# Q, K and V of three chunks as 64-row matmul pairs inside the gate-up stages of a fused adaLN, local-attention and GLU block

## Chip, cores and metric

The kernel runs on one core of one Trainium2 chip. The metric is the device time of one execution in microseconds (us). Three runs of the kernel before took 559.21, 559.87 and 560.19 us; the median is 559.87.

## What is computed

```python
x = A_x                                          # 1 x 2048 x 576, bfloat16
mod = (silu(c) @ w_mod).reshape(1, 6, 1, 576)
sa, ca, ga, sb, cb, gb = mod[:, 0], ..., mod[:, 5]
h = layernorm(x) * (1 + ca) + sa
q, k, v = h @ wqkv                               # 32 heads of 18
# each position attends to 8 positions: itself and those 2, 4, ... 14 before it
attn = softmax(mask(q . k[pos - 2*w] * 18**-0.5))
x = x + ga * ((attn . v[pos - 2*w]) @ wo)
h = layernorm(x) * (1 + cb) + sb
x = x + gb * (((h @ w_gate) * (h @ w_up)) @ w_down)   # 576 -> 4608 -> 576
```

## The kernel before

The 2048 rows are 8 chunks of 256 (`CH`), or 16 tiles of 128. The attention half works by chunks; the feed-forward half works by five groups of tiles, `GROUPS = [(0, 2), (2, 6), (6, 10), (10, 13), (13, 16)]` (L42). The width 576 is held as four blocks of 128 rows and one of 64 (`KF`, index 4).

**The stages.** After a prologue (chunk 0, and Q, K, V of chunks 1 and 2) the loop at L1066 runs, for each group `gi`, `gate_up(gi)` (L651) and then `down(gi)` (L713). In the texts, "gate-up 1" is the gate-up stage of group 1, the second one. PE carries the stage's own matmuls; the attention of later chunks is woven in as *pieces*, small functions that issue some instructions. Each engine runs its instructions in the order in which the code issues them: the schedule is written by hand. `spread` (L641) places the pieces over the loop by their weights: a piece goes to the loop count `f` in which the middle of its weight falls.

**Gate-up** (L651 to L700) loops over 36 blocks `f` of 128 of the 4608 columns. For each it forms a gate tile `pg` and an up tile `pu`, each in a PSUM bank of its own. It uses matmuls with 64 rows of contraction: one on the array's lower 64 rows and one on its upper 64 rows run at the same time. 576 rows are nine halves of 64, so each tile takes nine 64-row matmuls. `first_part(f)` issues five pairs: lower rows write `pg`, upper rows `pu`; the odd half comes from `wgr`, which holds the last 64 weight rows of gate in its lower and those of up in its upper half. `second_part(f)` issues the other four pairs with the banks swapped. Before it a wait makes sure that the last matmul of the first part has landed, as the two halves must not write one bank together (L676). The order is `first_part(f)`, `second_part(f - 1)`, the pieces of `f`, `product(f - 1)`, so that a first part lies between the two parts of one `f`. ACT copies `pu` and `pg` to `u_sb` and `g_sb` (L683, L684, three buffers each); DVE multiplies them into `hh` (L688). `ahead` (L702) asks for the weight block two blocks on, on SP's queue.

**Down** (L713 to L779) loops over the same 36 blocks and accumulates, for each tile `j` of the group, a 512-wide matmul into `acc` (L726) and a 64-wide one into `accr` (L730). The first 32 loops carry pieces, all of weight 1. The `wd` blocks come by POOL's queue, three buffers. The outputs are scaled, added and stored at the end.

**A chunk's attention, in pieces.**
- `a_ln`, `a_norm` (L337, L342): statistics on DVE, `rsq` on ACT (Ln, Exp), the norm on DVE into `ln_xn`. The norm also writes the last 64 columns a second time, beside the first copy.
- `a_t` (L357), called T: ten PE transposes into two banks, then scale and shift on DVE and ACT into `hT`.
- `a_q` (L386): Q and K as nine tiles of 128 columns, five full-array matmuls of 256 columns each (L376); ACT copies them to `qT` and `kT`, of which there are two sets, and copies 16 halo columns of the chunk before (`a_halo`). The fifth block of Q and of K share one tile, with weights `wq4`.
- `a_v` (L394): V for each of two tiles, five matmuls 504 wide and five 72 wide; ACT copies them with the order of head and element exchanged (`v_sb`), and POOL's queue writes them to DRAM (`vd`). In the fifth block of rows the upper 64 weight rows are zero.
- `b_ld` (L412): POOL's queue reads eight shifted copies of V back from DRAM.
- `b_p`, `b_lq`, `b_lt`, `b_sm0`, `b_sm1`: products of Q and shifted K on DVE, sums over a head on PE, transposes, softmax. `b_mul`, `b_add`: weighted sum of V on DVE.
- `b_o`, `b_w`, `b_ln`, `b_norm`, `b_t`: transposes, `wo`, residual, second norm, transposes into `h2T`, which the next gate-up reads.

**Where they stand.** Gate-up 1, 2 and 3 carry the middle of the attention of chunks 3 and 4, 5 and 6, and 7 (`gbg`, L1041). A down stage carries, from `out_qkv(i, n)` (L630), the end of chunk `i` mixed with the norm, T, Q, K and V of chunk `n`. Down 0 does so for n = 3 and 4, down 1 for n = 5 and 6, down 2 for n = 7 (`dbg`, L1062). `load_x(n + 2)` on SP's queue stands behind `a_norm(n)`.

**PSUM.** All tiles share one pool of eight banks; a tile waits until its bank's former tile has been read.

Of the kernel before, what the change touches and what calls it, by code (L numbers as in the profile page):

```python
# [7 lines left out]
BF = mybir.dt.bfloat16  # L8
# [30 lines left out]

MODK = (0, 4, 1, 2, 3)  # L40
QKK = (0, 1, 4, 2, 3)
GROUPS = [(0, 2), (2, 6), (6, 10), (10, 13), (13, 16)]  # L42


@with_exitstack
def kernel(
# [47 lines left out]
    def js(j):  # L94
        return slice(j * P, (j + 1) * P)
# [193 lines left out]
    def transposed(src, dst, cols, vi, between=None):  # L289
        n = P * len(cols)  # L290
        pA = ps([P, 3, n], BF, "tr_pA")
        pB = ps([P, 2, n], BF, "tr_pB")
        for c, j in enumerate(cols):
            if c and between:
                between()
            for m in range(KT):
                d = pA[:, m, :] if m < 3 else pB[:, m - 3, :]
                nc.tensor.transpose(d[:, js(c)], src[:, j, m * P:(m + 1) * P], ident[:])  # L298

        def evict(on_dve=(0, 1, 2)):  # L300
            for m in range(KT):
# [55 lines left out]
    def a_t(i, on_dve=(0, 1, 2), between=None):  # L357
        a_tiles(i)
        hT = aa[i]["hT"]
        transposed(aa[i]["xn"], lambda m: hT[:, m, :], (0, 1), 0, between)(on_dve)  # L360

    def qk_w(kt, m):
        if m == KF:
# [80 lines left out]
    def b_lt(i):  # L444
        b = bb[i]
        lgs = b.pop("lgs")
        pt = ps([P, 2, ST, P], BF, "lt")
        for a in range(2):
            for j in range(ST):
                nc.tensor.transpose(pt[:, a, j, :], lgs[:, a, js(j)], ident[:])  # L450
        nc.scalar.copy(b["lgt"][:].rearrange("p a j w h -> p (a j w h)"), pt[:].rearrange("p a j n -> p (a j n)"))

    def b_sm0(i):
        b = bb[i]
        lg = b.pop("lgt")
        mx = smp.tile([P, ST, 4, H], BF, name="mx", tag="tree")
        dd = smp.tile([P, 2, ST, 4, H], F32, name="dd")
        nc.vector.tensor_tensor(mx[:], lg[:, 0], lg[:, 1], ALU.max)
        nc.vector.tensor_tensor(mx[:, :, 0:2], mx[:, :, 0:2], mx[:, :, 2:4], ALU.max)
        nc.vector.tensor_tensor(mx[:, :, 0], mx[:, :, 0], mx[:, :, 1], ALU.max)  # L460
        for wq in range(2):
            nc.vector.tensor_tensor(dd[:, wq], lg[:, wq], mx[:, :, 0:1].to_broadcast([P, ST, 4, H]), ALU.subtract)
        nc.scalar.activation(dd[:], dd[:], ACTF.Exp, scale=scale)
        b["dd"] = dd
# [32 lines left out]
    def b_o(i):  # L497
# [8 lines left out]
            nc.scalar.copy(oT[:, m:m + 2, :], pA[:, m:m + 2, :])  # L506
        nc.scalar.copy(oT[:, 4, :], pB[:, 0, :])

    keyed = []

    def to_keys(j):
# [102 lines left out]
    def B_two(a, b, av_a, av_b):  # L614
        return (B_pr(a, 0, 6) + B_lq(a, 0) + B_pr(a, 6, 8) + B_pr(b, 0, 2) + B_lq(a, 1) + B_pr(b, 2, 6) + B_lq(b, 0) + B_sm(a)
                + B_pr(b, 6, 8) + av_a[:4] + B_lq(b, 1) + av_a[4:] + B_sm(b) + av_b)

    def B_one(a, av_a):
        return B_pr(a, 0, 6) + B_lq(a, 0) + B_pr(a, 6, 8) + B_wait(1.5) + B_lq(a, 1) + B_wait(4.0) + B_sm(a) + av_a

    def B_av(i):
        r = []
# [6 lines left out]

    def out_qkv(i, n):  # L630
        o = [lambda: b_o(i), lambda: b_w(i, 0), lambda: b_w(i, 1), lambda: b_ln(i), lambda: b_norm(i), lambda: b_t(i, (0,) if i == 6 else (0, 1))]
        if n >= NCH:
# [15 lines left out]
        return at  # L648


    def gate_up(gi, hh, bg):  # L651
        N = P * (GROUPS[gi][1] - GROUPS[gi][0])
        ht = h2T[gi]
        at = spread(bg, FT)
        lo, hi = slice(0, 64), slice(64, P)
        pgu = {}

        def half(bank, lhs, rhs, first, last):
            return nc.tensor.matmul(bank[:, 0:N], lhsT=lhs, rhs=rhs, start=first, stop=last, skip_group_check=True)  # L659

        def first_part(f):
            wb = wgu_blk[gi * NBLK + f // FB]
            cs = slice((f % FB) * P, (f % FB + 1) * P)
            pg, pu = ps([P, 2 * CH], F32, "pg"), ps([P, 2 * CH], F32, "pu")
            half(pg, wgr[lo, js(f)], ht[lo, KF, 0:N], True, False)
            half(pu, wgr[hi, js(f)], ht[hi, KF, 0:N], True, False)
            for k in range(KF):
                half(pg, wb[lo, k, 0, cs], ht[lo, k, 0:N], False, False)
                m = half(pu, wb[hi, k, 1, cs], ht[hi, k, 0:N], False, False)
            pgu[f] = (pg, pu, m)  # L670

        def second_part(f):
            wb = wgu_blk[gi * NBLK + f // FB]
            cs = slice((f % FB) * P, (f % FB + 1) * P)
            pg, pu, m = pgu.pop(f)
            swap = nc.tensor.nop()  # L676
            tc.add_manual_dep(swap.ins, m.ins.name, SYNC, reason="row tiles swap banks")
            for k in range(KF):
                half(pu, wb[lo, k, 1, cs], ht[lo, k, 0:N], False, k == KF - 1)
                half(pg, wb[hi, k, 0, cs], ht[hi, k, 0:N], False, k == KF - 1)  # L680
            g = gup.tile([P, 2 * CH], BF, name="g_sb")
            u = gup.tile([P, 2 * CH], BF, name="u_sb")
            nc.scalar.copy(u[:, 0:N], pu[:, 0:N])  # L683
            nc.scalar.copy(g[:, 0:N], pg[:, 0:N])  # L684
            return g, u

        def product(f, gu):
            nc.vector.tensor_tensor(hh[:, f, 0:N], gu[0][:, 0:N], gu[1][:, 0:N], ALU.mult)  # L688

        for f in range(FT):  # L690
            first_part(f)
            gu = second_part(f - 1) if f > 0 else None
            if f > 0 and f % FB == 0:
                ahead(gi, f // FB)
            for piece in at[f]:
                piece()
            if gu:
                product(f - 1, gu)
        product(FT - 1, second_part(FT - 1))
        ahead(gi, NBLK)  # L700

    def ahead(gi, n):  # L702
# [352 lines left out]
    def gb_row():  # L1055
# [3 lines left out]
        b_ld(2, 1)  # L1059
        load_wd(2)  # L1060

    dbg = {0: [gb_row] + first + out_qkv(2, 4),  # L1062
           1: out_qkv(3, 5) + out_qkv(4, 6),
           2: out_qkv(5, 7) + out_qkv(6, 8),
           3: [nop, lambda: b_t(6, (1,))] + out_qkv(7, 8)}
    for gi in range(NG):  # L1066
        if gi == 1:
            hh0_guard.__exit__(None, None, None)
            wgx_guard.__exit__(None, None, None)
            hhp = pool("hhp", 1)  # L1070
        hh = hhp.tile([P, FT, 2 * CH], BF, name="hh") if gi else hh0
        gate_up(gi, hh, gbg.get(gi, []))
        down(gi, hh, dbg.get(gi, []))


# [28 lines left out]
```

## Time and profile before

| | |
|---|---|
| median of three runs | 559.87 us |
| profiled execution | 560.52 us |
| its span, first to last instruction | 558.7 us |
| granted PE clock | 1.00 |
| gate-up 0, down 0 | 49.7 to 92.0, 92.0 to 133.5 us |
| gate-up 1, down 1 | 133.5 to 207.4, 207.4 to 266.05 us |
| gate-up 2, down 2 | 266.05 to 339.9, 339.9 to 390.2 us |
| gate-up 3, down 3 | 390.2 to 445.0, 445.0 to 475.4 us |
| gate-up 4, down 4 | 475.4 to 528.15, 528.15 to 558.7 us |

All times within the trace are in us from the start of the span. The engines are PE (matmuls; PEld is its weight loads), DVE, ACT, POOL and SP. In the rows by instruction the first number is the start, the second the duration. A matmul's duration runs until its results have landed, so durations of matmuls in a row overlap: the time that one takes from PE's stream is the distance from its start to the next start. `64*128 64x512` means 64 contraction rows, 128 columns of weights, and 512 columns streamed.

### The profile page before, as it was taken

How to read it: one execution, taken by the hardware profiler on the slowest of the kernel's cores; microseconds unless marked ns; L12 is line 12 of the kernel's file. 1: busy time of each engine (PE TensorE's matmuls, PEld its weight loads, DVE VectorE, ACT ScalarE, POOL GpSimd, SP SyncE). 2: the span in 40 equal slices, each digit the busy share in tenths (PEclk: the TensorE clock that was granted, in tenths of full speed). 3: DMA queues.
4: the chain of work that ended last, by engine and by line, in shares of the span. 5: the costliest groups of instructions: out<-in, count | busy, mean ns of one | idle time of the engine just before them, and what ended most of it. 6: DMA issues, size and time to landing. Idle time of an engine off the chain costs nothing.

```text
span 558.7 us, 14224 instructions
## 1 busy us (share of the span) xinstructions
PE 547.8 (98%) x5972; PEld 325.0 (58%) x6012; DVE 331.2 (59%) x796; ACT 250.6 (45%) x584; POOL 63.4 (11%) x97
## 2 busy tenths in 40 slices
PE   7999999999999999999999999999999999999997
PEld 4887796665444446656444445655565555555564
DVE  7888798984777776252858686406736614322202
ACT  2746666354465652323355654230466511456500
POOL 3103101123000001111100000111100022000020
PEclk9999999999999999999999999999999999999999
DMA  8999999645646745233834855234965565565053
GB/s 271 282 292 309 340 306 352 193 147 177 230 143 218 247 141 166 92 101 106 288 119 152 276 174 182 86 106 128 324 195 192 185 194 177 182 193 187 1 170 117
DMA packets 69994, 108.14 MB, mean 194 GB/s; under 512 B 3658, under 2 KB 57754, under 8 KB 69930
## 3 DMA queue, kind: packets, MB, share of 16 engines
q1 hardware_dynamic: 58672, 61.28, 35.2%
q0 software_dynamic: 11168, 45.81, 25.4%
q8 instruction: 47, 0.77, 0.6%
q14 instruction: 17, 0.14, 0.1%
q10 hardware_dynamic: 90, 0.15, 0.1%
HBM read 102.78 MB, written 4.44 MB: 192 GB/s over the span
## 4 chain that ended last, share of the span: by engine, by line
PE 84%; DMA 10%; issue 3%; SPq 1%; DVE 1%; POOL 0%; POOLq 0%
PE pg L659 26%; PE pu L659 21%; PE acc L726 20%; PE pq L376 4%; PE accr L730 4%; DMA wgr<-in_B_w_gate_dram 3%; PE pw L577 2%; PE pv L399 2%; DMA wo<-in_A_wo_dram 2%; DMA wgu<-in_B_w_up_dram 2%; DMA x_t<-in_A_x_dram 2%; PE lg L434 2%; DMA wd<-in_B_w_down_dram 1%; SPq L150 1%; DMA wmA<-in_w_mod_dram 1%
## 5 line engine op out<-in xcount | busy, mean ns | idle before, releaser
L659 PE MATMUL pg<-h2T,wgu 64*128 64x512 bf16 (+2 forms) x1440 | 277.3, 333 | 0.0
L659 PE MATMUL pu<-h2T,wgu 64*128 64x512 bf16 (+2 forms) x1440 | 275.8, 333 | 0.0
L659 PEld LDWEIGHTS <-wgu 64*128 64x128 bf16 x2880 | 142.8, 94 | 105.7 <-issue 0.5
L683 ACT CAST u_sb<-pu 128x512 bf16<-128x512 f32 (+2 forms) x180 | 90.2, 501 | 136.3 <-PE pg L659 134.7
L726 PE MATMUL acc<-wd,hh 128*128 128x512 bf16 (+1 forms) x554 | 140.2, 369 | 0.8 <-DMA wd<-in_B_w_down_dram 0.5
L688 DVE TENSOR_TENSOR hh<-g_sb,u_sb 128x512 bf16<-128x512 bf16 (+2 forms) x180 | 66.7, 372 | 99.3 <-ACT g_sb L684 97.8
L730 PE MATMUL accr<-wd,hh 128*128 128x64 bf16 x576 | 99.2, 193 | 1.6
L684 ACT CAST g_sb<-pg 128x512 bf16<-128x512 f32 (+2 forms) x180 | 91.3, 507 | 0.0
L726 PEld LDWEIGHTS <-hh 128*128 128x128 bf16 x588 | 55.3, 98 | 57.1 <-issue 1.7
L165 POOL DMA_DIRECT2D wd<-in_B_w_down_dram x45 | 33.9, 753 | 292.6 <-PE accr L730 270.5
L659 PE MATMUL pu<-h2T,wgr 64*128 64x512 bf16 (+2 forms) x180 | 60.2, 335 | 0.3 <-ACT u_sb L683 0.3
L659 PE MATMUL pg<-h2T,wgr 64*128 64x512 bf16 (+2 forms) x180 | 60.2, 335 | 0.2 <-DVE h2T L285 0.2
L730 PEld LDWEIGHTS <-hh 128*128 128x128 bf16 x576 | 51.7, 98 | 2.6 <-issue 0.7
L424 DVE TENSOR_TENSOR prod<-qT,kT 128x1280 bf16<-128x1280 bf16 x56 | 44.7, 818 | 2.5 <-PE lg L434 2.5
L484 DVE TENSOR_TENSOR vsh<-vsh,attn 128x1152 bf16<-128x1152 bf16 x56 | 41.0, 750 | 0.0
L285 DVE TENSOR_SCALAR h2T<-tr_pA,modc 128x256 bf16<-128x256 bf16 (+1 forms) x27 | 8.8, 382 | 36.8 <-PE tr_pA L298 36.8
L376 PE MATMUL pq<-hT,wqk 128*128 128x256 bf16 x240 | 30.0, 273 | 0.0
L376 PEld LDWEIGHTS <-wqk 128*128 128x128 bf16 x280 | 25.7, 98 | 4.8
L659 PEld LDWEIGHTS <-wgr 64*128 64x128 bf16 x360 | 18.1, 94 | 16.8 <-issue 4.5
L418 POOL DMA_DIRECT2D vsh<-vd x14 | 12.5, 892 | 123.3 <-DVE o_sb L495 84.4
L579 DVE TENSOR_TENSOR x<-pw,ga_bc 128x512 bf16<-128x512 f32 x14 | 9.7, 689 | 22.4 <-PE pw L577 22.1
L379 ACT CAST qT<-pq 128x512 bf16<-128x512 f32 x14 | 8.1, 581 | 28.3 <-PE pq L376 28.3
(196 smaller groups left out, 489.9 us busy)
## 6 DMA issues: line engine op xcount, KB each, us to landing
wd<-in_B_w_down_dram POOLq DMA_DIRECT2D x45, 576.0 KB, 4.4
wgu<-in_B_w_gate_dram SPq DMA_DIRECT2D x45, 512.0 KB, 4.0
wgu<-in_B_w_up_dram SPq DMA_DIRECT2D x45, 512.0 KB, 5.6
vsh<-vd POOLq DMA_DIRECT2D x14, 1152.0 KB, 8.9
x_r<-in_A_x_dram SPq DMA_DIRECT2D x8, 288.0 KB, 6.4
out_dram<-x SPq DMA_DIRECT2D x15, 144.0 KB, 5.4
x_t<-in_A_x_dram SPq DMA_DIRECT2D x7, 288.0 KB, 5.8
vd<-v_sb POOLq DMA_DIRECT2D x14, 144.0 KB, 3.1
```

The source lines that it names most:

```text
L165: return nc.gpsimd.dma_start(wb[:], B_w_down[r0:r0 + FB * P, :].rearrange("(k p) n -> p k n", p=P))
L376: nc.tensor.matmul(pq[:, gi, :], lhsT=qk_w(kt, m), rhs=hT[:, kt, cols], start=(kt == 0), stop=(kt == KT - 1))
L399: nc.tensor.matmul(pv[:], lhsT=hT[:, kt, js(j)], rhs=wv[:, kt, 0:VA * DH], start=(kt == 0), stop=(kt == KT - 1))
L418: return nc.gpsimd.dma_start(vsh[:].rearrange("p w d h -> p w (d h)"), vsrc)
L424: nc.vector.tensor_tensor(prod[:], aa[i]["qT"][:], aa[i]["kT"][:, :, off:off + CH], ALU.mult)
L484: nc.vector.tensor_tensor(v, v, at, ALU.mult)
L659: return nc.tensor.matmul(bank[:, 0:N], lhsT=lhs, rhs=rhs, start=first, stop=last, skip_group_check=True)
L683: nc.scalar.copy(u[:, 0:N], pu[:, 0:N])
L684: nc.scalar.copy(g[:, 0:N], pg[:, 0:N])
L688: nc.vector.tensor_tensor(hh[:, f, 0:N], gu[0][:, 0:N], gu[1][:, 0:N], ALU.mult)
L726: nc.tensor.matmul(a[:], lhsT=hh[:, f, js(j)], rhs=wb[:, f % FB, cs], start=(f == 0), stop=(f == FT - 1))
L730: nc.tensor.matmul(accr[:, j, :], lhsT=hh[:, f, js(j)], rhs=wb[:, f % FB, 512:D], start=(f == 0 and j == 0), stop=(f == FT - 1), skip_grou ...
```

## The change

For chunks 5, 6 and 7 (`PAIRED`) Q, K and V leave the down stages and are formed in gate-up 1, 2 and 3 as 64-row pairs.

- `load_pair_rows`, a new last piece of down 0, loads the last 64 rows of the Q/K and V weights a second time, into the upper halves of the fifth block, which were zero; POOL rebuilds the upper half of that block of `wq4`, and ACT writes two columns of `modc` so that T of a paired chunk fills the upper half of `hT`'s fifth block as well.
- A chunk has five *units*, each in two parts like a gate-up tile: Q (two tiles of 256 in each of two banks, 18 pairs), K (the same), the shared Q/K tile (9 pairs of 128), and two of V (9 pairs of 288 each; lower and upper rows work on the chunk's two tiles). The second part ends with the ACT copies, and with the DRAM writes for V.
- `gate_up` now works through a list of items, gate-up tiles and units: the first part of an item, then the second part of the item before. Chunk 5's units stand behind f = 29 to 33 of gate-up 1, chunk 6's behind f = 0 to 4 of gate-up 2, chunk 7's behind f = 0 (three), 1 and 2 of gate-up 3, whose pieces start at f = 2. Its read of chunk 7's values stands behind the fourth `b_p`.
- `a_ln(5)`, `a_norm(5)` and `load_x(7)` move from down 1 into gate-up 1, behind the attention of chunk 3, and T of chunk 5 stands between `b_lt(4)` and `b_sm0(4)`.
- In down 1 and 2 `out_qkv` keeps the norm and T of chunks 6 and 7 and fills with empty pieces.

```diff
+PAIRED = (5, 6, 7)
...
-    modc = consts.tile([P, 4, KT], F32, name="modc")
+    modc = consts.tile([P, 4, KT + 1], F32, name="modc")
...
-                modulate(dst(m), s, m, vi + 1, vi, m in on_dve)
+                modulate(dst(m), s, kf if m == KF else m, vi + 1, vi, m in on_dve)
...
+    def swap_after(m):
+        swap = nc.tensor.nop()
+        tc.add_manual_dep(swap.ins, m.ins.name, SYNC, reason="row tiles swap banks")
+
+    def load_pair_rows():
+        nc.sync.dma_start(wqk[64:, KF, :], A_wqkv[KF * P:D, 0:2 * D])
+        nc.sync.dma_start(wv[64:, KF, :], A_wqkv[KF * P:D, 2 * D:3 * D])
+        nc.gpsimd.tensor_copy(halves(wq4[64:, KF, :]), halves(wqk[64:, KF, :])[:, :, KF * P:D])
+        for r in (LO, HI):
+            nc.scalar.copy(modc[r, 0:2, KT], modc[0:64, 0:2, KF])
+
+    def pair_unit(width, tiles, evict):
+        st = {}
+
+        def first():
+            banks = [ps([P, len(tiles), width], F32, "pp") for _ in range(2)]
+            for t, ops in enumerate(tiles):
+                for k in (KF, 0, 1, 2, 3):
+                    for bank, rows, op in zip(banks, (LO, HI), ops):
+                        lhs, rhs = op(k)
+                        m = half(bank[:, t, :], lhs[rows], rhs[rows], t == 0 and k == KF, False)
+            st.update(banks=banks, m=m)
+
+        def second():
+            banks = st["banks"]
+            swap_after(st["m"])
+            for t, ops in enumerate(tiles):
+                for k in range(KF):
+                    for bank, rows, op in zip(banks[::-1], (LO, HI), ops[::-1]):
+                        lhs, rhs = op(k)
+                        half(bank[:, t, :], lhs[rows], rhs[rows], False, k == KF - 1)
+            evict(*banks)
+        return first, second
+
+    def qkv_units(i, plan):
...
+        units = ([pair_unit(CH, [(qk_op(m), qk_op(m + 2)) for m in (0, 1)], q_out),
+                 pair_unit(CH, [(qk_op(m), qk_op(m + 2)) for m in (KT, KT + 1)], k_out),
+                 pair_unit(P, [(qk_op(KF, js(0)), qk_op(KF, js(1)))], qk4_out)]
+                + [pair_unit(288, [(v_op(0, hf), v_op(1, hf))], v_out(hf)) for hf in range(2)])
+        return {f: units[a:b] for f, a, b in plan}
...
-    def B_sm(i):
-        return [(0.5, lambda: b_lt(i)), (1.2, lambda: b_sm0(i)), (0.6, nop), (1.8, lambda: b_sm1(i))]
+    def B_sm(i, turned=None):
+        return [(0.5, lambda: b_lt(i))] + ([(1.0, lambda: a_t(turned))] if turned else []) + [ (1.2, lambda: b_sm0(i)), (0.6, nop), (1.8, lambda: b_sm1(i))]
...
+        if n in PAIRED:
+            return [lambda: a_ln(n), o[0], lambda: (a_norm(n), load_x(n + 2)), o[1], lambda: a_t(n), o[2], o[3], nop, o[4], nop, nop, o[5]]
...
+        items = []
         for f in range(FT):
-            first_part(f)
-            gu = second_part(f - 1) if f > 0 else None
...
+            items += [(lambda f=f: first_part(f), lambda f=f: second_part(f))] + units.get(f, [])
+        for k, (first, _) in enumerate(items):
+            first()
+            for piece in items[k - 1][1:] if k else at[0]:
                 piece()
...
+        items[-1][1]()
...
-           1: values(3) + B_two(3, 4, B_av(3) + [res(3), res(4)], B_av(4)),
+           1: values(3) + B_two(3, 4, B_av(3) + [res(3), res(4), (2.4, lambda: a_ln(5)), (1.2, lambda: (a_norm(5), load_x(7)))], B_av(4), 5),
            2: values(5) + B_two(5, 6, B_av(5) + [res(5), res(6)], B_av(6)),
-           3: values(7) + B_one(7, B_av(7)) + [res(7)]}
+           3: B_one(7, values(7), B_av(7)) + [res(7)]}
...
-    dbg = {0: [gb_row] + first + out_qkv(2, 4),
+    dbg = {0: [gb_row] + first + out_qkv(2, 4) + [load_pair_rows],
...
+    units = {1: qkv_units(5, [(29, 0, 1), (30, 1, 2), (31, 2, 3), (32, 3, 4), (33, 4, 5)]),
+             2: qkv_units(6, [(0, 0, 1), (1, 1, 2), (2, 2, 3), (3, 3, 4), (4, 4, 5)]),
+             3: qkv_units(7, [(0, 0, 3), (1, 3, 4), (2, 4, 5)])}
```

More of the change, by code (lines that the diff above doesn't have):

```diff
@@ L287, in modulate, with transposed @@
             nc.scalar.activation(dst, s, ACTF.Identity, bias=modc[:, vi_shift, m:m + 1], scale=modc[:, vi_scale, m:m + 1])
-    def transposed(src, dst, cols, vi, between=None):
+    def transposed(src, dst, cols, vi, between=None, kf=KF):
         n = P * len(cols)
@@ L359, in a_t @@
         hT = aa[i]["hT"]
-        transposed(aa[i]["xn"], lambda m: hT[:, m, :], (0, 1), 0, between)(on_dve)
+        transposed(aa[i]["xn"], lambda m: hT[:, m, :], (0, 1), 0, between, KT if i in PAIRED else KF)(on_dve)
     def qk_w(kt, m):
@@ L507, in b_o, with half @@
         nc.scalar.copy(oT[:, 4, :], pB[:, 0, :])
+    LO, HI = slice(0, 64), slice(64, P)
+    def half(dst, lhs, rhs, first, last):
+        return nc.tensor.matmul(dst, lhsT=lhs, rhs=rhs, start=first, stop=last, skip_group_check=True)
+    def swap_after(m):
[7 more added lines that the diff above has]
+            nc.scalar.copy(modc[r, 0:2, KT], modc[0:64, 0:2, KF])
@@ new lines, in qkv_units, with qk_op, v_op, q_out @@
+    def qkv_units(i, plan):
+        qT, kT = qTs[i % 2], kTs[i % 2]
+        vs = []
+        def qk_op(m, cols=slice(0, CH)):
+            return lambda k: (qk_w(k, m), aa[i]["hT"][:, k, cols])
+        def v_op(j, hf):
+            return lambda k: (aa[i]["hT"][:, k, js(j)], wv[:, k, 288 * hf:288 * (hf + 1)])
+        def q_out(a, b):
+            nc.scalar.copy(qT[:, 0:2, :], a[:])
+            nc.scalar.copy(qT[:, 2:4, :], b[:])
+        def k_out(a, b):
+            nc.scalar.copy(kT[:, 0:2, HALO:], a[:])
+            nc.scalar.copy(kT[:, 2:4, HALO:], b[:])
+        def qk4_out(a, b):
+            for j, t in enumerate((a, b)):
+                nc.scalar.copy(kT[0:64, KF, HALO + j * P:HALO + (j + 1) * P], t[64:P, 0, :])
+                nc.scalar.copy(qT[:, KF, js(j)], t[:, 0, :])
+            a_halo(i)
+        def v_out(hf):
+            def out_(a, b):
+                for j, t in enumerate((a, b)):
+                    if hf == 0:
+                        vs.append(vstage.tile([P, DH, H], BF, name="v_sb"))
+                    nc.scalar.copy(vs[j][:, :, 16 * hf:16 * (hf + 1)], t[:, 0, :].rearrange("p (h d) -> p d h", d=DH))
+                    if hf == 1:
+                        r0 = HALO + i * CH + j * P
+                        nc.gpsimd.dma_start(vd[r0:r0 + P, :], vs[j][:].rearrange("p d h -> p (d h)"))
+            return out_
+        units = ([pair_unit(CH, [(qk_op(m), qk_op(m + 2)) for m in (0, 1)], q_out),
[3 more added lines that the diff above has]
+        return {f: units[a:b] for f, a, b in plan}
@@ L648, in spread, with gate_up @@
         return at
-    def gate_up(gi, hh, bg):
+    def gate_up(gi, hh, bg, units={}, bg_from=0):
         N = P * (GROUPS[gi][1] - GROUPS[gi][0])
         ht = h2T[gi]
-        at = spread(bg, FT)
-        lo, hi = slice(0, 64), slice(64, P)
+        at = [[] for _ in range(bg_from)] + spread(bg, FT - bg_from) + [[]]
         pgu = {}
-        def half(bank, lhs, rhs, first, last):
-            return nc.tensor.matmul(bank[:, 0:N], lhsT=lhs, rhs=rhs, start=first, stop=last, skip_group_check=True)
         def first_part(f):
@@ L664, in first_part @@
             pg, pu = ps([P, 2 * CH], F32, "pg"), ps([P, 2 * CH], F32, "pu")
-            half(pg, wgr[lo, js(f)], ht[lo, KF, 0:N], True, False)
-            half(pu, wgr[hi, js(f)], ht[hi, KF, 0:N], True, False)
+            half(pg[:, 0:N], wgr[LO, js(f)], ht[LO, KF, 0:N], True, False)
+            half(pu[:, 0:N], wgr[HI, js(f)], ht[HI, KF, 0:N], True, False)
             for k in range(KF):
-                half(pg, wb[lo, k, 0, cs], ht[lo, k, 0:N], False, False)
-                m = half(pu, wb[hi, k, 1, cs], ht[hi, k, 0:N], False, False)
+                half(pg[:, 0:N], wb[LO, k, 0, cs], ht[LO, k, 0:N], False, False)
+                m = half(pu[:, 0:N], wb[HI, k, 1, cs], ht[HI, k, 0:N], False, False)
             pgu[f] = (pg, pu, m)
@@ L675, in second_part @@
             pg, pu, m = pgu.pop(f)
-            swap = nc.tensor.nop()
-            tc.add_manual_dep(swap.ins, m.ins.name, SYNC, reason="row tiles swap banks")
+            swap_after(m)
             for k in range(KF):
-                half(pu, wb[lo, k, 1, cs], ht[lo, k, 0:N], False, k == KF - 1)
-                half(pg, wb[hi, k, 0, cs], ht[hi, k, 0:N], False, k == KF - 1)
+                half(pu[:, 0:N], wb[LO, k, 1, cs], ht[LO, k, 0:N], False, k == KF - 1)
+                half(pg[:, 0:N], wb[HI, k, 0, cs], ht[HI, k, 0:N], False, k == KF - 1)
             g = gup.tile([P, 2 * CH], BF, name="g_sb")
@@ L684, in second_part @@
             nc.scalar.copy(g[:, 0:N], pg[:, 0:N])
-            return g, u
-        def product(f, gu):
-            nc.vector.tensor_tensor(hh[:, f, 0:N], gu[0][:, 0:N], gu[1][:, 0:N], ALU.mult)
-        for f in range(FT):
-            first_part(f)
-            gu = second_part(f - 1) if f > 0 else None
-            if f > 0 and f % FB == 0:
-                ahead(gi, f // FB)
-            for piece in at[f]:
+            if f < FT - 1 and f % FB == FB - 1:
+                ahead(gi, f // FB + 1)
+            for piece in at[f + 1]:
+                piece()
+            nc.vector.tensor_tensor(hh[:, f, 0:N], g[:, 0:N], u[:, 0:N], ALU.mult)
+        items = []
+        for f in range(FT):
+            items += [(lambda f=f: first_part(f), lambda f=f: second_part(f))] + units.get(f, [])
+        for k, (first, _) in enumerate(items):
+            first()
+            for piece in items[k - 1][1:] if k else at[0]:
                 piece()
-            if gu:
-                product(f - 1, gu)
-        product(FT - 1, second_part(FT - 1))
+        items[-1][1]()
         ahead(gi, NBLK)
@@ L1071 @@
         hh = hhp.tile([P, FT, 2 * CH], BF, name="hh") if gi else hh0
-        gate_up(gi, hh, gbg.get(gi, []))
+        gate_up(gi, hh, gbg.get(gi, []), units.get(gi, {}), 2 if gi == 3 else 0)
         down(gi, hh, dbg.get(gi, []))
```

10 lines of the change are left out of this document (5 added, 5 removed).

## The prediction

> **What bounds the kernel now.** I read the shares and the chain of waits first, then the busy time by stage, then single instructions in order of time.
>
> ```profile
> PE 547.8 (98%) x5972; PEld 325.0 (58%) x6012; DVE 331.2 (59%) x796; ACT 250.6 (45%) x584; POOL 63.4 (11%) x97
> ...
> PE 84%; DMA 10%; issue 3%; SPq 1%; DVE 1%; POOL 0%; POOLq 0%
> ```
>
> PE is 84% of the chain that ended last; the DMA share lies in the first 100 us. So time is a sum of PE streaming, if nothing in the stages concerned makes PE wait. By stage (start:end, span, then busy us of PE, PEld, DVE, ACT, POOL):
>
> ```profile
> 133.50:207.40 73.90, 73.90 (x738) 33.18 (x738) 55.31 (x109) 40.38 (x76) 4.31 (x5) 1.00 0.61 201
> 207.40:266.05 58.65, 58.12 (x510) 35.55 (x522) 25.07 (x70) 18.88 (x47) 8.24 (x12) 1.00 0.37 115
> ```
>
> These are gate-up 1 and down 1. PE is never idle in gate-up 1, at granted clock 1.00; DVE and ACT have 18 and 33 us free in it. Busy does not mean gap-free, since a matmul's row is longer than its stream, so I compared start-to-start times: gate-up 1 has only its 36 x 9 pairs, 4 `b_lq` blocks and 2 `b_lt` blocks, with about 0.09 us at each change between 64-row and full-array matmuls; no wait for data shows.
>
> **Removed.** Nine Q/K tiles of 5 matmuls and V's 20, per chunk, from down 1 (chunks 5, 6) and down 2 (chunk 7):
>
> ```profile
> 114.69 0.45 PE oT_pA L504 x8
> ...
> 219.05 1.09 PE pq L376 x10
> ```
> ```profile
> 231.22 1.23 PE L399 MATMUL pv<-wv,hT 128*128 128x504 bf16 x5
> 232.28 0.33 PE L401 MATMUL pvr<-wv,hT 128*128 128x72 bf16 x5
> ```
>
> Q/K: 1.09/10 = 0.109 us each, x45 = 4.91. V wide: (232.28 - 231.22)/5 = 0.212, x10 = 2.12. V narrow: 0.33 less one row of 0.197 (its group's mean) is four steps, 0.033 each, x10 = 0.33. Together 7.36 us a chunk, all on the PE stream. The first line (the chain, as the second) gives a 128-wide transpose: 0.45/8 = 0.056.
>
> **Added.** 576 rows are nine 64-row halves; run two at a time they are 4.5 passes instead of 5. The price of a 256-wide pair is seen in gate-up 0, whose tiles are 256 wide (pg and pu start together; the `wgr` pair opens each group of nine):
>
> ```profile
> 53.22 0.27 PE L659 MATMUL pg<-h2T,wgr 64*128 64x256 bf16 x1
> 53.24 0.27 PE L659 MATMUL pu<-h2T,wgr 64*128 64x256 bf16 x1
> ...
> 54.20 0.27 PE L659 MATMUL pg<-h2T,wgr 64*128 64x256 bf16 x1
> 54.22 0.27 PE L659 MATMUL pu<-h2T,wgr 64*128 64x256 bf16 x1
> ```
>
> Nine pairs in 54.20 - 53.22 = 0.98 us: 0.109 a pair, weight loads hidden. Q and K take four 9-pair tiles, 36 x 0.109 = 3.92. V's pairs are 288 wide, which gate-up does not have. They lie between the 256-wide pair, 0.109, and the 512-wide one, 0.216 (182.19 to 182.41 in gate-up 1); full-array rows last 273 ns at 256 wide and 288 ns at 288 wide (means of `pq` and `pwj`), so I take 0.109 + 0.014 = 0.123: 18 x 0.123 = 2.21. The last Q/K tile has nine pairs of 128. No row shows such a pair: at best the stream of one 128-wide matmul, 0.056, at worst two in a row, 0.112. In 0.056 two loads and two matmuls must issue; the down stage issues one load and one 64-wide matmul in 0.03 (accr at 232.66, acc at 232.69), about that rate. I take 0.056: 0.50. Sum 6.63 a chunk, 0.73 less than what goes; three chunks: -2.19 us. At 0.112 the sum loses 1.5 of that.
>
> Units stand between gate-up tiles of the same 64-row form, so no change of form is added. By the trace one costs:
>
> ```profile
> 182.41 0.38 PE L659 MATMUL pu<-h2T,wgu 64*128 64x512 bf16 x1
> ...
> 182.72 0.40 PE L450 MATMUL lt<-ident,lgs 128*128 128x128 bf16 x4
> 183.05 0.39 PE L659 MATMUL pg<-h2T,wgr 64*128 64x512 bf16 x1
> ```
>
> Four transposes at 0.056 are 0.22 of the 0.33 from 182.72; 0.1 is the change back. The ten transposes of T(5) follow `b_lt(4)` directly, so they use its two changes; they cost 0.56 in either stage.
>
> Each second half waits until the last matmul of its first half has landed. Between the two lies the first half of the next item. With 256-wide pairs that is 0.55 us and gate-up 0 shows no gap; only behind a 128-wide unit is it 5 x 0.056 = 0.28, against a 512-wide matmul's 0.38 row. 0 to 0.1 in each of three places; I take 0.1 in all.
>
> **Norm and T of chunk 5.** The pieces fall, by the middles of their weights (29.38, 31.18, 32.03 and 32.78 of 47.68, times 36), to f = 22 (`a_ln`), 23 (`a_norm`, `load_x(7)`) and 24 (`b_lt(4)`, then T). Rows to price it, from down 1 and gate-up 1:
>
> ```profile
> 208.99 0.81 DVE L253 BATCH_NORM_STATS2 ln_statsa<-x_t 128x6 f32<-128x288 bf16 x2
> ...
> 210.76 0.21 DVE L255 BATCH_NORM_AGGREGATE ln_mva<-ln_statsa 128x2 f32<-128x12 f32 x1
> 211.76 1.28 DVE L263 TENSOR_SCALAR ln_xn<-x_t,ln_mva,ln_rstda 128x576 bf16<-128x576 bf16 x4 [0.78 <-ACT ln_rstda L259]
> ```
> ```profile
> 182.82 0.59 ACT L683 CAST u_sb<-pu 128x512 bf16<-128x512 f32 x1 [0.87 <-PE pg L659]
> 183.30 0.59 ACT L684 CAST g_sb<-pg 128x512 bf16<-128x512 f32 x1
> ```
>
> Let E be the end of the second half of f = 22 on PE; nine pairs of 0.216 later, 1.94 us, the next ends. In the trace before this half's stream ended at 182.41 + 0.22 = 182.63, so u's copy starts at E+0.19 and ACT is free at E+1.15. `rsq` stands behind these copies and takes 0.59 to the first norm (211.17 to 211.76): norms run E+1.74 to E+3.02. DVE reaches them in time: `a_ln` (1.98) and product 21 end at E+0.1. PE reaches the transposes at E+1.94+0.31; the second five start 0.28 later, at E+2.53, and their rows of `ln_xn` come at about E+3.05. PE waits 0.5 us. It is 0 if `rsq` slips ahead, 1.3 (all four norms bare) if DVE is a little later; I take 0.5. Behind the waiting transposes stands gate-up itself. What is late next is product 22, 0.6 behind its usual place; three buffers of u and g absorb it.
>
> `load_x(7)` moves on SP's queue in front of two weight loads and waits for the norm, about 1 us; those weights are for f = 32 and are asked for at f = 24.
>
> **The rest, at nothing, and its cover.** `load_pair_rows` adds two small loads on SP in front of down 0's stores, two tiny ACT copies, and a POOL copy (0.3, the earlier ones) that waits for the first load, some 3 us (144 KB landed in 3.1). Behind it on POOL stand one `wd` load and chunk 3's values, needed at f = 13, about 25 us later. V rows go to DRAM later, yet `b_ld(5)` is issued at the next stage as before, and `b_ld(7)` at f = 6 for use at f = 22, 23 us for a 8.9 us load. In down 1 the `wd` blocks are used faster, 4 x 0.98 us each, against 4.4 us to landing with three buffers. The chain `b_w`, norm, `b_t` before each gate-up has 7 loops of 0.98 between its last `b_w` and its `b_t` and needs about 5.5. Of three waits of 0.15 between pwr and pw (down 1 twice, down 2) one loses its cause, the bank of T(5): -0.15, or 0.
>
> **Sum:** -2.19 + 0.1 + 0.5 - 0.15 = -1.74 us. Against the profiled execution (560.52, span 558.7 and 1.8 around it) 558.8; that execution is 0.65 above the median of 559.87, so in terms of the median **558.1**.
>
> **Rivals.**
> *Narrow pairs do not overlap.* Two loads and two matmuls do not fit into one 128-wide stream, so each 128-wide matmul takes 0.056 alone: +1.5, sum -0.24, **559.6**. For it: no row shows the pair, and its issue rate is the tightest seen. Against: accr (0.03) and the `b_lq` blocks (20 in 0.66) issue nearly as fast. The Trainium skill, TensorE: Matmul & The Clock Gate, Back-to-back issue gap, gives 81 ns for a sustained 128-wide load and matmul; by it these units take 18 x 81 ns = 1.46 us a chunk, +2.9 in all, an estimate of 561.0. The transposes here step at 56 ns, so the trace does not bear that figure out for full-array matmuls.
>
> *Evictions end last (the slower side).* Each unit adds two to five ACT copies (512 wide 0.48 apart, 256 wide 0.37 each, halo 0.26). If ACT falls behind, the next item waits for its PSUM bank. From 0.12 us per unit the 15 units eat the gain; from 0.19 the kernel is slower by over 0.2%; at 0.25, +3.75, sum +2.0, **561.9**. For it: V units with four copies, about 1.6 us (0.37 at 256 wide, 0.58 at 504), beside a gate-up tile's 0.96 in 1.94 + 1.1 us of PE, 84% busy; in the built order one bank is reused after only ten pairs. Against: most come back after 18 pairs or more, and ACT has 33 us free in gate-up 1. The Trainium skill, TensorEngine Tiling (Array Packing), PSUM Bottleneck, warns that tiling speeds TensorE but not the emptying of PSUM; in gate-up 1, tiled throughout, ACT waits for PE before every u copy (0.87), which agrees only so far as PE is the slower here.
>
> *The halves of a unit run one after the other*, for a reason gate-up does not show: 6.6 more a chunk, near 578.
>
> **How the numbers follow.** Forecast 0.65, narrow pairs 0.20, evictions 0.12, serial halves 0.03. The forecast's own range is from no wait at T(5) (-2.4, 557.5) to 1.3 there and no gain at pw (-0.8, 559.1), with the runs' spread of 0.5 around it. The range 557.1 to 560.3 takes in the narrow pairs too. What runs of this kernel tell from no change is about 0.2%, 1.1 us. Most of the forecast's chance lies beyond that, a part and nearly all of the narrow pairs within: faster 0.58, same 0.29, slower 0.13.
>
> **What would show it.** Down 1 should last about 58.65 - 2 x 7.36 - 0.56 - 0.15 = 43.2 us, down 2 42.9; gate-up 1 73.9 + 6.63 + 0.56 + 0.5 = 81.6 and gate-up 2 and 3 6.6 more each. `pp` pairs should start 0.109, 0.123 and 0.056 apart. PE should wait for `ln_xn` once, near f = 24. Wrong would be: 128-wide pairs 0.11 apart, PE idle behind ACT at a unit's or tile's first matmul, a longer wait at T(5), or a tail of down 1 waiting for `b_t(4)`.

## The result, and the profile after

The changed kernel took 558.69 us in the median (557.45 to 559.92, 17 runs), the kernel before 559.84 us beside it (559.21 to 560.74, 17 runs). The ratio is 0.9979, 95% interval 0.9972 to 0.9986: faster by 1.15 us, where 1.74 was forecast. The profiled execution took 559.92 us, its span is 558.2 us.

Busy time of the engines and the chain that ended last, from the page of the changed kernel:

```profile
PE 548.4 (98%) x6195; PEld 323.7 (58%) x6195; DVE 330.1 (59%) x796; ACT 251.3 (45%) x592; POOL 63.2 (11%) x98
...
PE 56%; issue 27%; DMA 4%; POOL 2%; DVE 1%; ACT 0%; POOLq 0%; SPq 0%; ACTq 0%
```

The 27% "issue" looks like a new limit and is none. The chain follows inferred releasers, and it books the same kernel differently from one execution to the next. Another execution of it (`r_after2`) has this chain:

```profile
PE 82%; DMA 11%; issue 4%; DVE 1%; SPq 1%; POOL 1%; ACT 0%; POOLq 0%
```

PE sets the time in both, so stage lengths on PE tell where the time went. Gate-up 1 and down 1 by windows (start:end, span, then busy us of PE, PEld, DVE, ACT, POOL):

```profile
133.28:214.57 81.29, 81.24 (x874) 39.47 (x873) 58.64 (x122) 46.37 (x93) 5.40 (x7) 1.00 0.60 196
214.57:257.79 43.22, 43.22 (x380) 23.49 (x379) 20.72 (x57) 8.44 (x21) 6.01 (x8) 1.00 0.44 136
```

Down 1 lost 15.4 us and gate-up 1 gained 7.4; ACT is still 35 us short of the span in gate-up 1, the granted clock is 1.00. The stages, from the first matmul of one to the first of the next, in us:

| stage | before | after | change | forecast |
|---|---|---|---|---|
| gate-up 1 | 73.87 | 81.29 | +7.42 | 81.6 |
| down 1 | 58.65 | 43.22 | -15.43 | 43.2 |
| gate-up 2 | 73.87 | 80.50 | +6.63 | +6.6 |
| down 2 | 50.31 | 42.94 | -7.37 | 42.9 |
| gate-up 3 | 54.76 | 62.38 | +7.62 | +6.6 |
| down 4 | 30.64 | 31.43 | +0.79 | 0 |

The other stages moved by 0.1 or less. Two rows stand out. Down 4 had one late `wd` block in this execution; none of the later profiles of this or a like kernel shows one of this size (30.46 to 30.59), so it belongs to this execution. Gate-up 3 is 1.0 us longer than the units explain.

**The units cost what was forecast.** PE by time, gate-up 2 (start, us, what; rows of one kind are drawn together, with their number):

```profile
258.88 1.25 PE L513 MATMUL pp<-hT,wqk 64*128 64x256 bf16 x20
259.97 0.38 PE L513 MATMUL pu<-h2T,wgu 64*128 64x512 bf16 x1
...
266.69 0.44 PE L513 MATMUL pp<-hT,wq 64*128 64x128 bf16 x10
266.98 0.38 PE L513 MATMUL pu<-h2T,wgu 64*128 64x512 bf16 x1
...
268.92 0.39 PE L513 MATMUL pp<-hT,wq 64*128 64x128 bf16 x8
269.14 0.78 PE L513 MATMUL pp<-wv,hT 64*128 64x288 bf16 x10
269.75 0.38 PE L513 MATMUL pu<-h2T,wgu 64*128 64x512 bf16 x1
```

Starts divided by pairs: 1.09/10 = 0.109 for 256 wide, 0.28/5 = 0.056 for 128 wide (unrounded 266.695 to 266.975; 0.22/4 again in the second half), 0.61/5 = 0.123 for 288 wide. No gap stands at a swap of banks, and none behind ACT.

**T(5) waits 0.2 us.** PE, then DVE, then ACT of gate-up 1 (in brackets: idle time before, and its releaser):

```profile
184.71 0.33 PE L299 MATMUL tr_pA<-ident,ln_xn 128*128 128x128 bf16 x3
184.88 0.28 PE L299 MATMUL tr_pB<-ident,ln_xn 128*128 128x128 bf16 x2
185.21 0.34 PE L299 MATMUL tr_pA<-ident,ln_xn 128*128 128x128 bf16 x3
```

```profile
184.17 1.19 DVE L264 TENSOR_SCALAR ln_xn<-x_t,ln_mva,ln_rstda 128x576 bf16<-128x576 bf16 x4 [1.70 <-ACT ln_rstda L260]
```

```profile
183.60 0.31 ACT L259 ACTIVATE ln_rstda<-ln_mva,eps 128x2 f32<-128x2 f32 x1
183.94 0.20 ACT L260 ACTIVATE ln_rstda<-ln_rstda 128x2 f32<-128x2 f32 x1
```

The second five transposes would start two steps of 0.056 after 184.88, at 184.99; they start at 185.21, so the wait is 0.22 us. The group of four norms runs until 185.36; PE was let go behind the third of them (the second tile's 576 columns, from 184.72 for 0.43), since the fourth only writes the 64 columns that the last transpose reads.

**Gate-up 3 has a wait that was not forecast.** PE, at the first block of f = 16:

```profile
412.33 0.32 PE L513 MATMUL pg<-h2T,wgu 64*128 64x384 bf16 x1
413.34 0.33 PE L513 MATMUL pu<-h2T,wgu 64*128 64x384 bf16 x1 [0.69 <-DMA wgu<-in_B_w_up_dram]
```

A `pu` starts beside its `pg`; this one starts 1.01 us later, because the up weights are late, and all of that is lost. For one pair step, 0.16 us, the other half of the array still has work, so nothing starts at all for the other 0.85; the expectations below call these 0.85 the wait and the 0.16 one step more. From here `pu` runs that step behind `pg`, until the full-array transposes of `b_lt`, which come when both halves are done: from the `wgr` row of f = 17 to these transposes is 1.71 us here (414.49 to 416.20) and 1.56 in a kernel without the lag (413.54 to 415.10, `e1_v_first` below). 62.38 less 1.01 is 61.37; `e1_v_first` has 61.36, the stage of before plus 6.60.

Two transfers run beside this. POOL's and SP's queues in the changed kernel:

```profile
393.98 1.11 POOL L581 DMA_DIRECT2D vd<-v_sb  x2 [11.63 <-ACT v_sb L578]
398.32 1.80 POOL L419 DMA_DIRECT2D vsh<-vd  x2 [3.23 <-DVE prod L425]
```

```profile
401.04 1.78 SPq L151 DMA_DIRECT2D wgu<-in_B_w_up_dram  x1
```

Chunk 7's V rows are written at 394, its values (twice 1152 KB) asked for at 398.3, and the weights of f = 16 just behind, the gate half at 400.62 and the up half at 401.04. Before, the values were asked for at 391.26. That gives the theories for the runs. *A*: the values, now later, lie in front of this weight block in the transfers and make it late. *B*: the block is late by chance or for another reason (V's writes, the order of units). Beside that it had to be shown that the gain is the pairing's.

### The profile page after: what moved, and what is told of

Read it like the earlier page. It is cut to its first block, busy times and chain, and to the rows that moved or that the text cites. A ratio compares the mean times of both kernels' runs of the same rounds, so it can differ in the third digit from the quotient of the medians.

```text
span 558.2 us, 14633 instructions
## 1 busy us (share of the span) xinstructions
PE 548.4 (98%) x6195; PEld 323.7 (58%) x6195; DVE 330.1 (59%) x796; ACT 251.3 (45%) x592; POOL 63.2 (11%) x98
## 4 chain that ended last, share of the span: by engine, by line
PE 56%; issue 27%; DMA 4%; POOL 2%; DVE 1%; ACT 0%; POOLq 0%; SPq 0%; ACTq 0%
PE pg L513 16%; PE acc L803 13%; PE pu L513 13%; PE pp L513 4%; DMA wd<-in_B_w_down_dram 2%; PE pw L658 2%; PE accr L807 2%; POOL wd L166 2%; PE pq L377 2%; DMA wgu<-in_B_w_up_dram 2%; PE lg L435 1%; PE pv L400 1%; PE tr_pA L299 1%; POOL vsh L419 1%; PE oT_pA L505 0%
## 5 line engine op out<-in xcount | busy, mean ns | idle before, releaser
L803 PE MATMUL acc<-wd,hh 128*128 128x512 bf16 (+1 forms) x588 | 142.7, 370 | 0.5 <-DMA wd<-in_B_w_down_dram 0.4
L259 ACT ACTIVATE ln_rstdb<-ln_mvb,eps 128x2 f32<-128x2 f32 (+1 forms) x9 | 2.7, 296 | 44.0 <-DVE ln_mvb L256 44.0
L288 ACT ACTIVATE h2T<-tr_pB,modc 128x256 bf16<-128x256 bf16 (+1 forms) x16 | 7.7, 533 | 30.2 <-PE tr_pB L299 30.2
L492 DVE TENSOR_TENSOR vsh<-vsh 128x1152 bf16<-128x1152 bf16 x28 | 20.5, 752 | 0.0
```

What stands on the lines that cost most here:

```text
L492: nc.vector.tensor_tensor(vsh[:, d], vsh[:, d], vsh[:, 4 + 2 * s:6 + 2 * s], ALU.add)
L803: nc.tensor.matmul(a[:], lhsT=hh[:, f, js(j)], rhs=wb[:, f % FB, cs], start=(f == 0), stop=(f == FT - 1))
```

## The experiments

In every set the kernel before ran on the same chip; its median was 560.05 us in the set of `r_after` and `e1` to `e3`, 559.90 in that of `e4` to `e6` and `e1_again`, 559.66 in that of `e7`, `e8` and `r_after2`, and 560.08 beside `e9`.

### The changed kernel again (`r_after`, `r_after2`)

> The changed kernel once more, for a second profile. Theory A: in gate-up 3 the values of chunk 7 (2.3 MB, now asked for 17 us into the stage instead of 1.3 us) lie in front of a weight block, and PE waits for that block near f = 16: 0.3 to 2 us there again, time near 558.7. Theory B: late landings by chance, not bound to a place (down 4 had one of 0.87 us too): the wait in gate-up 3 is gone or elsewhere in this profile, time near 558.7 all the same.

> The changed kernel beside the two others: 558.5 to 558.9 us; values sent at about 398 us; a wait at the block of f = 16 between 0 and 0.85 us, and gate-up 3 61.4 plus that wait plus 0.16 if there is one.

558.91 us (ratio 0.998, 0.9968 to 0.9992) and 558.60 us (0.9988, 0.9971 to 1.0004). By its times the second set alone does not tell the kernel from the one before. Gate-up 3 lasted 61.99 with `pu` 0.62 late at f = 16, and 61.58 with 0.21. The lag is in every profile of this schedule, at the same block, in changing size; down 4's is not.

### V first (`e1_v_first`, `e1_again`)

```diff
+        if i == 7:
+            units = units[3:] + units[:3]
...
-        return B_pr(a, 0, 4) + ld + B_pr(a, 4, 6) + ...
+        return ld + B_pr(a, 0, 6) + ...
...
-             3: qkv_units(7, [(0, 0, 3), (1, 3, 4), (2, 4, 5)])}
+             3: qkv_units(7, [(0, 0, 5)])}
```

> Chunk 7's two V units go first, all five units stand behind f = 0 of gate-up 3, and the values are asked for ahead of the first product, some 7 us earlier than in the changed kernel. PE work is the same. Theory A: no wait for weights in gate-up 3, gain near the 1.74 us of the forecast: 0.6 us under the changed kernel, 558.1 (557.7 to 558.4). Theory B: as the changed kernel, 558.7, waits at other places.

> The same kernel as e1_v_first, run beside the three others on one chip, to compare e6_norm_earlier with: 557.7 to 558.2 us, ratio 0.9965 to 0.9975, no DMA wait of PE in gate-up 3.

557.96 us (0.9971, 0.9961 to 0.9982) and 557.90 us (0.9966, 0.9955 to 0.9978). POOL asks for the values eight us earlier:

```profile
390.49 1.80 POOL L419 DMA_DIRECT2D vsh<-vd  x2 [2.56 <-DMA vd<-v_sb]
```

Gate-up 3 lasts 61.36 in both, with no wait for weights. That agrees with A, but the units' order was changed too.

### The values in two steps, and their place later in the code (`e2_split`, `e5_values_later`)

```diff
-        return B_pr(a, 0, 4) + ld + B_pr(a, 4, 6) + ... + B_lq(a, 1) + B_wait(4.0) + ...
+        return B_pr(a, 0, 4) + ld[:1] + B_pr(a, 4, 6) + ... + B_lq(a, 1) + B_wait(2.4) + ld[1:] + B_wait(1.6) + ...   # e2
+        return B_pr(a, 0, 6) + B_lq(a, 0) + B_pr(a, 6, 8) + ld + B_wait(1.5) + ...                                     # e5
...
-           3: B_one(7, values(7), B_av(7)) + [res(7)]}
+           3: B_one(7, [(0.0, lambda j=j: b_ld(7, j)) for j in range(ST)], B_av(7)) + [res(7)]}                           # e2
```

> Of chunk 7's two value loads only the first stands where the changed kernel has both; the second (1.15 MB, needed at f = 29) moves behind the second sum of the logits, near f = 13. Theory A: each burst is half as long, the wait near f = 16 is gone or below 0.2 us: 558.1 to 558.4. Theory B: 558.7.

> As the changed kernel, but the read of chunk 7's values stands behind the eighth b_p and not behind the fourth, about four loops of 1.6 us later in gate-up 3. Theory A (the values' 2.3 MB in two bulk loads hold up the weight block asked for beside them): the wait at the block of f = 16 goes, and comes back at the block or two whose loads now meet the values (f = 20 or 24), with 0.4 to 0.9 us; time as the changed kernel, 558.4 to 559.2. Theory B (block 16's weights come late for another reason, as chance or the new V writes): the wait stays at f = 16 (413 us) or is seen nowhere.

558.58 us (0.9983, 0.9967 to 0.9999) and 558.50 us (0.9976, 0.9966 to 0.9987). Neither edit did what it was meant to: POOL asked for both values together at 398.10 and at 398.55, as without it. POOL's queue holds nothing else there, so the place among the pieces delays nothing; the request goes out when V's rows have landed in DRAM (2.90 and 3.68 us after POOL had issued the writes; the profile names this landing in four of five executions of the schedule, and in the first a DVE product that ends at about the same time). As tests of A both are void. As two more executions of the changed schedule they show `pu` 0.23 and 0.46 late at f = 16, gate-up 3 61.60 and 61.83.

### Chunk 7 left in down 2 (`e3_chunk7_down`)

```diff
-PAIRED = (5, 6, 7)
+PAIRED = (5, 6)
...
-        return B_pr(a, 0, 4) + ld + B_pr(a, 4, 6) + ...
+        return ld + B_pr(a, 0, 6) + ...
...
-             3: qkv_units(7, [(0, 0, 3), (1, 3, 4), (2, 4, 5)])}
...
-        gate_up(gi, hh, gbg.get(gi, []), units.get(gi, {}), 2 if gi == 3 else 0)
+        gate_up(gi, hh, gbg.get(gi, []), units.get(gi, {}))
```

> Chunks 5 and 6 as in the changed kernel; chunk 7's Q, K and V stay in down 2 and its values are asked for at the start of gate-up 3, as before. Pairs save 2 x 0.73 = 1.46 us, T(5) costs 0.2, one pw wait is gone. Theory A: no weight wait in gate-up 3, so 1.4 us under before, 558.4: within 0.3 of the changed kernel, as chunk 7's 0.73 was all but eaten by the wait. Theory B: the changed kernel less chunk 7's gain, 558.7 + 0.73 = 559.4.

558.53 us (0.9972, 0.9962 to 0.9983). Values at 390.30, no wait, gate-up 3 54.72 and down 2 50.31 as before. So as the change puts chunk 7, its pairing bought nothing that these runs can tell (558.91 with it). With V first the stages show what it is worth: down 2 and gate-up 3 together last 104.30 there and 105.03 here. The total times do not resolve this (ratios 0.9971 and 0.9972).

### The same places without pairing (`e4_whole`)

Each unit's products as full-array matmuls; `load_pair_rows` is left out, so that the upper rows of the fifth weight block stay zero.

```diff
-                for k in (KF, 0, 1, 2, 3):
-                    for bank, rows, op in zip(banks, (LO, HI), ops):
-                        lhs, rhs = op(k)
-                        m = half(bank[:, t, :], lhs[rows], rhs[rows], t == 0 and k == KF, False)
+                for k in (KF, 0, 1, 2, 3):                # one bank in each part of the unit
+                    lhs, rhs = ops[which](k)
+                    half(bank[:, t, :], lhs, rhs, t == 0 and k == KF, k == KF - 1)
```

> The units stand where the change puts them, but each product is a full-array matmul of 128 rows, as in the kernel before (nine pairs become ten full-array matmuls per Q/K tile of two; the upper rows of the fifth weight block stay zero, so load_pair_rows is left out). If the gain comes from pairing and not from the place, this must be slower than before. By the prediction's prices each chunk's products cost 7.36 instead of 6.63, and each of the 17 stretches of full-array matmuls between 64-row ones costs two changes of form at about 0.09 us: +2.2 + 3.1 = +5.3 on the changed kernel, so about 564 us, ratio about 1.007. Rival (the gain comes from moving the work out of down, where something else made it dear): then the time stays near 559 or at most rises by the changes of form, below 562.

563.37 us (1.0065, 1.0046 to 1.0084). Gate-up 1 and 2 are 2.01 and 2.02 us longer than with pairs: 0.73 for the products and 12 changes of form at about 0.1. Gate-up 3 is 63.16, 1.80 more than without a lag. Moved work alone makes the kernel 3.5 us slower; the gain is the pairing's. That it needs neighbours of the same form is an estimate: 12 changes at about 0.1 us would cost more than the 0.73 that pairs save in a chunk, but no run has pairs among full-array matmuls.

### The values held (`e7_held_late`, `e8_first_held`)

These move the request itself: it is made to wait for a DVE product. In `e7` that is the eighth `b_p`'s in the changed kernel, in `e8` the fifth's in the kernel with V first.

```diff
+        last_prod[0] = nc.vector.tensor_tensor(prod[:], ...)          # in b_p
...
+        if i == 7:                                                     # in b_ld
+            tc.add_manual_dep(ld.ins, last_prod[0].ins.name, SYNC, reason="held")
...
+        return B_pr(a, 0, 6) + B_lq(a, 0) + B_pr(a, 6, 8) + ld + ...   # e7
+        return B_pr(a, 0, 5) + ld + B_pr(a, 5, 6) + ...                # e8
```

> As the changed kernel, but the two reads of chunk 7's values are made to wait for the product of the eighth b_p, which ends at about 403 us, and so go out about 5 us later, behind the requests for the weights of f = 16 and not ahead of them. Theory A (values ahead of the weights in the rings make them late): no PE wait at f = 16 (412 us); gate-up 3 61.4 us, unless the next block's weights (asked for near 407, needed near 419) now land late instead. Theory B (the V writes, or chance, make f = 16 late): the wait at f = 16 stays at 0.1 to 0.85 us.

> As the kernel with V's units first and all five units behind f = 0, whose gate-up 3 had no wait for weights and lasted 61.36 us, but the two reads of chunk 7's values are made to wait for the product of the fifth b_p, which ends at about 398.1 us: they go out when the changed kernel sends them, and nothing else is moved. Theory A: the wait at the block of f = 16 comes back, 0.1 to 0.85 us and one pair step of 0.16 more behind it, gate-up 3 61.6 to 62.4, time near 558.5. Theory B (the order of the units was what mattered): gate-up 3 stays at 61.36 and the time at 558.0.

`e7`: 557.71 us (0.9966, 0.9954 to 0.9978). The request goes out behind the weights of f = 16:

```profile
402.76 1.80 POOL L421 DMA_DIRECT2D vsh<-vd  x2 [8.28 <-DVE prod L430]
```

There is no lag, gate-up 3 is 61.36. `e8`: 558.62 us (0.998, 0.9971 to 0.9989); the request goes out when the changed kernel sends it, with V's rows long in place, and the lag is back at the same block. POOL, then PE:

```profile
398.66 1.80 POOL L421 DMA_DIRECT2D vsh<-vd  x2 [10.48 <-DVE prod L430]
```

```profile
412.50 0.32 PE L518 MATMUL pg<-h2T,wgu 64*128 64x384 bf16 x1
413.18 0.33 PE L518 MATMUL pu<-h2T,wgu 64*128 64x384 bf16 x1 [0.36 <-DMA wgu<-in_B_w_up_dram]
```

`pu` is 0.68 late, and gate-up 3 is 62.05, 0.69 over 61.36. The time of the request takes the lag away and brings it back, whatever the order of the units. In all, the six profiles with the request between 397.85 and 398.66 have `pu` late at f = 16, and gate-up 3 is 61.36 plus this lag, to within 0.02 us, in each. The five that pair chunk 7 and send the request at another time (`e1_v_first`, `e1_again`, `e6`, `e7`, `e9`) have none, `e7` and `e9` with V's rows written as late as in the changed kernel. A holds, B falls.

How the values get in front is seen in the transfers from 400 to 403 us, when the weights of f = 16 are asked for. First the changed kernel, then `e7` (DMA queue: packets, MB, share of the 16 engines; then an issue, its size, and us to landing; q0 carries POOL's requests, q1 SP's):

```profile
q0 software_dynamic: 187, 0.86, 88.1%
q1 hardware_dynamic: 35, 0.03, 3.0%
...
wgu<-in_B_w_gate_dram SPq DMA_DIRECT2D x1, 512.0 KB, 11.2
```

```profile
q1 hardware_dynamic: 553, 0.56, 59.4%
...
wgu<-in_B_w_gate_dram SPq DMA_DIRECT2D x1, 512.0 KB, 3.6
```

The 35 packets of q1 in the changed kernel are the end of the block before. The weights asked for at 400.62 moved nothing before 404.3, and from then on shared with the values until these ran out at 410.6. From 405 to 407 us:

```profile
q0 software_dynamic: 136, 0.62, 82.7%
q1 hardware_dynamic: 125, 0.13, 19.5%
```

They landed 11.2 us after the request; in `e7`, alone, after 3.6. The up half was asked for at 401.04 and wanted 11.3 us later, at 412.33: no slack at all. In `e7` the next block's weights meet the values instead and take 8.0, which still fits.

### Without either wait (`e6_norm_earlier`, `e9_both`)

```diff
-B_av(3) + [res(3), res(4), (2.4, lambda: a_ln(5)), (1.2, lambda: (a_norm(5), load_x(7)))]
+B_av(3)[:13] + [(2.4, lambda: a_ln(5)), (1.2, lambda: (a_norm(5), load_x(7)))] + B_av(3)[13:] + [res(3), res(4)]
```

`e6` adds this to the kernel with V first, `e9` to `e7`.

> As the kernel with chunk 7's values asked for ahead of the first b_p and its five units behind f = 0, and with a_ln(5) and a_norm(5) three pieces earlier in gate-up 1, so that T(5) finds its rows ready. If T(5)'s wait is the 0.2 us that the trace shows, it goes: 0.2 us below the kernel without this step, about 557.8 against 558.0, gate-up 1 81.1 instead of 81.29, and no PE wait for ln_xn near 185 us. Rival: the norm's DVE work ahead of chunk 3's last sums delays them, and with them other pieces; then gate-up 1 or down 1 is longer by 0.3 or more.

> The changed kernel with both waits taken away that its trace shows: the reads of chunk 7's values held until the eighth b_p's product, and a_ln(5), a_norm(5) three pieces earlier in gate-up 1. By the stage sums: gate-up 1 81.06, gate-up 3 61.36, so 0.2 less than the kernel that is held alone: about 557.5, ratio about 0.9962. If the two steps disturb each other (weights late in another stage), gate-up 3 is again 61.6 or more.

`e6`: 558.09 us (0.9963, 0.9952 to 0.9975), beside `e1_again`'s 557.90. `e9`: 557.67 us (0.9961, 0.9947 to 0.9975). Gate-up 1 is 81.06 in both, 0.23 shorter, and T(5) runs through (PE, `e9`):

```profile
183.66 0.33 PE L299 MATMUL tr_pA<-ident,ln_xn 128*128 128x128 bf16 x3
183.83 0.28 PE L299 MATMUL tr_pB<-ident,ln_xn 128*128 128x128 bf16 x2
183.94 0.33 PE L299 MATMUL tr_pA<-ident,ln_xn 128*128 128x128 bf16 x3
```

Two tenths of a us are below what the total times resolve, so they show in the stage alone. `e9` has the least span of all, 555.0, with gate-up 3 at 61.36; but 1.4 of its 3.7 us below the kernel before lie ahead of gate-up 0, where the change has no part.

## Why the prediction came out as it did

Direction and mechanism were right, and the time lies in the forecast's own range. Two terms of the sum were too large, and one step that was priced at nothing was not nothing. That these nearly cancel (0.38 us too much, and 0.5 in the mean left out) is luck.

- *Pairs, -2.19.* As forecast to the third digit: 0.109, 0.123 and 0.056 a pair; gate-up 2 grew by 6.63, and down 1 and 2 shrank as said. The rival of narrow pairs that do not overlap (0.112) is out, and so is that of halves one after the other. The 81 ns that the Trainium skill, TensorE: Matmul & The Clock Gate, Back-to-back issue gap, gives for a 128-wide load and matmul is not borne out here either: two of each fit into 56 ns.
- *Swaps behind a 128-wide unit, +0.1.* No gap is seen.
- *T(5), +0.5.* Measured 0.22. The norms started 1.7 us after E, as worked out; the term was mis-sized because it let the second five wait for all four norms, and they wait for three.
- *`pw` waits, -0.15.* Down 1 lost one of two, as forecast.
- *Evictions on ACT.* PE waited for ACT at no unit; this rival is out for these widths.
- *The rest, at nothing.* This step failed, in its sentence on `b_ld(7)`: "issued at f = 6 for use at f = 22, 23 us for a 8.9 us load". It asked only whether the load comes in time for its own user. It does; but 2.3 MB moved from 391 to 398 us lie in front of the weights of f = 16, which have some 11 us from request to use: `pu` there came 0.21 to 1.01 us late. Nor is it the place among the pieces that sends the values, but the landing of V's rows in DRAM.

The trace of the kernel before had the sign. There the same values, asked for at 391.26, met the weights of f = 12, whose up half was asked for at 397.49 (391 to 403 us):

```profile
vsh<-vd POOLq DMA_DIRECT2D x2, 1152.0 KB, 11.5
...
wgu<-in_B_w_up_dram SPq DMA_DIRECT2D x1, 512.0 KB, 11.2
```

The two value loads took 11.5 us in the median, not the 8.9 of all fourteen, and the weights 11.2 of the 11.3 that they had: `pu` of f = 12 started at 408.79, 0.03 behind its `pg`. The slack in this stage was used up before the change.

With the measured 0.22 and no swap gaps the sum becomes -2.19 + 0.22 - 0.15 = -2.12; the stages without the weight wait add up to 7.42 - 15.43 + 6.63 - 7.37 + 6.60 = -2.15, and `e1` and `e7`, which have none, are 1.95 to 2.1 us below the kernel before by their medians, 1.6 to 1.9 by the ratios. The changed kernel gives part of this back. Five profiles of its schedule put gate-up 3 at 61.58 to 62.38, 0.2 to 1.0 over 61.36 and 0.5 in the mean, so by the stages it should gain 1.6; 1.15 was measured (0.8 to 1.6 by the interval). The medians beside `e1` and `e7` are 0.9 apart (558.91 and 557.96; 558.60 and 557.71), with intervals that overlap. So the wait is shown in place, cause and size, but not that it is the whole of the 0.9.

Open is why its size changes from run to run (0.21 to 1.01) with the request within 0.7 us of the same time. Open too is the spread of the times, 557.13 to 561.43 for the changed kernel in one set and 557.20 to 558.34 for `e7` in the same: a lag of at most 1.0 us, as profiled, does not account for it.

## What to carry to other kernels

Products that cannot fill the array can pay when they are paired among neighbours of the same form: the same work in the same places ended 1.1 us below the kernel before when paired and 3.5 us above it when not. When a step moves, follow its transfers past their own users: ask which request comes right behind each on the shared engines, and how much slack that one has. Where one bulk transfer meets a stream of weights just in time, try holding it until behind the next request: here that took the whole lag away.

## What the runs showed of the hardware that was not expected

- Transfers of two queues shared by packets and not by bytes, and not at once. In the changed kernel, 401 to 403 us, 147 packets of the values moved and none of the weights asked for at 400.62, which began at 404.3; in `e7`, 406 to 410 us, it was 331 to none. With no values in transit the weights began 1.0 us after the request (`e7`, 400.01). From 405 to 407 it was 136 to 125 packets, but 0.62 to 0.13 MB, since a packet of the values has 4608 bytes and one of the weights 1024. The Trainium skill, DMA: Bandwidth & Descriptors, Queues, rings and completion order, says that an engine takes turns between queues packet by packet. The counts from 405 to 407 agree with that; why the weights had no turn for the first 3.7 us, no run here shows.
- A late operand of one half of the array does not stop the other half at once: it ran one step (0.16 us) ahead, until a full-array matmul had to wait for both. The step is not won, as the stage lost the whole lag of the late half (1.01 of 1.02 us in the changed kernel).
- Two 64-row matmuls of 128 columns together step at 56 ns, no more than one full-array matmul of that width.
